# A transformer block's gradients on one core: the second norm made again in the tail, filters loaded twice, three pairs of w_down turned by TensorE

## The chip, the cores and the metric

The kernel runs on one core of a Trainium2 chip. The metric is the time of one execution on the device in microseconds. Five engines appear: TensorE (PE, with its weight loads as PEld), VectorE (DVE), ScalarE (ACT), GpSimd (POOL) and SyncE (SP). SP and POOL issue all of the kernel's transfers (DMAs).

## The reference

All data are bf16: 2048 tokens (S) of width 576 (D), a hidden width of 4608 (F).

```python
sa, ca, ga, sb, cb, gb = six rows of (silu(c) @ w_mod)
h = layernorm(x) * (1 + ca) + sa
x = x + ga * irfft2(rfft2(h) * (w_r + 1j * w_i))       # x1 below
h = layernorm(x) * (1 + cb) + sb                        # the second norm
x = x + gb * (((h @ w_gate) * (h @ w_up)) @ w_down)
```

The kernel gives this block's output and, for a given grad_out, the gradients of x, w_r, w_i, w_gate, w_up, w_down, c and w_mod. Both norms are over the 576 elements of a token. The filters w_r and w_i have 2048 x 289 elements.

## The kernel before, in words

Tokens are taken in 16 tiles of 128 (t), the hidden width in 36 blocks of 128 (fb). Four parts follow one another.

**Head** (0 to 62 us of the profile): loads, first norm, first transforms of the spectral filter. The two filters are loaded into one SBUF tile wn (L520, L521), whose rows are padded from 289 to 292 by a memset, and the padded tile is stored to a DRAM scratch wn_d (L524) for the tail.

**u4 and the forward filter** (62 to 268 us): u4 is (grad_out x gb) times w_down transposed, 36 blocks of four groups (function `u4_group`). PE needs w_down with its 576 columns on the partitions. So two blocks of w_down rows at a time (a pair k, 18 in all, buffer wdn, two of them) are loaded by SP (`wd_load`, L375 and L376) and turned by a DMA transpose, also from SP (`wd_turn`, L380, tile wdT). The groups of u4 are dealt between the steps of the filter (its stages 2 and 3); the blocks from 23 on run alone, at 4.1 us each, with the last 64 of 576 columns ahead (L549) and the others after them (L554). Stage 3 makes x1, stores it, and makes the second norm pair by pair of token tiles (`s3_norm`): ACT scales x1 to n2 (L669), DVE makes h2 from it in h2p (L671 to L673), POOL stores n2 (L674) to a scratch n2_d for the tail. Each four token tiles, SP transposes h2p to h2T by DMA (L677), which the main loop reads. n2 is laid out as six parts of 96 columns with two ones after each (98 wide, and padding to 608); with the ones, a matmul against it also gives column sums.

**Main loop** (268 to 1231 us): the 36 blocks of gate, up and their gradients.

**Tail** (1231 us on): in stage 1 the gradient goes back through the second norm (`t1_norm`, `norm_back`), one token tile a step, 16 steps of 4.0 us. SP loads n2 (tile n2c, five buffers) and y (yc, three buffers) of each tile (L1089). In `t1_turn`, `t1_cols` and `t1_rows` PE transposes (trp), and makes two transforms (zp, vp), with ACT copying each result out of PSUM (gyT, zt, b_Vp); csA, csB and csC gather the sums for the gradients of the modulation. The projection by w_down (u3p, L1394) is dealt between these steps and the later ones; its weights wd and its inputs hl are loaded as memory comes free (`queued_load`), by POOL and SP. Stage 2 multiplies by the filter, which POOL loads back from wn_d (L1176), with Xn, the stored spectrum, for the filter gradients (gwt, L1234). Stage 3 goes back to tokens and through the first norm.

The order on PE and ACT in the tail is written out by hand (`deal`, `in_order`). On SP and POOL a scheduler orders the instructions by priorities; `behind` and `queued` add an order between named instructions. Each queue issues in order: an instruction that waits holds all that stand behind it on its engine.

Of the kernel before, what the change touches and what calls it, by code (L numbers as in the profile page):

```python
# [10 lines left out]
BF = mybir.dt.bfloat16  # L11
# [14 lines left out]
DN = 608  # L26
# [64 lines left out]
def build(ctx, tc, A_x, A_w_r, A_w_i, B_w_gate, B_w_up, B_w_down, c_in, w_mod, grad_out,  # L91
# [25 lines left out]
    wn_d = dram("wn_d", [128, 2 * NT * FP], BF)  # L117
    n1_d = dram("n1_d", [128, NT, D], BF)
    n2_d = dram("n2_d", [128, NT, DN], BF)
# [7 lines left out]
    rstd2g = glob.tile([128, NT], FP32, name="rstd2g")  # L127
    dsl_col = glob.tile([128, 5], FP32, name="dsl_col")
# [5 lines left out]
    def part(ap):  # L134

        return ap[:, 0:6 * (DS if ap.shape[-1] == DN else DC)].rearrange("p (m c) -> p m c", m=6)[:, :, 0:DC]

    def parts(ap):

        return ap[:, :, 0:6 * (DS if ap.shape[-1] == DN else DC)].rearrange("p t (m c) -> p t m c", m=6)[:, :, :, 0:DC]  # L140
# [5 lines left out]
    def ones_between(ap):  # L146

        nc.gpsimd.memset(ap[:, :, 0:6 * DS].rearrange("p t (m c) -> p t m c", c=DS)[:, :, :, DC:DS], 1.0)
        nc.gpsimd.memset(ap[:, :, 6 * DS:DN], 1.0)
# [30 lines left out]
    def norm_stats(xt, pool, nt, name, rstd_out, room=None):  # L180
# [9 lines left out]
        nmr = pool.tile([128, room or nt], FP32, name=name + "_nmr")  # L190
        nc.vector.scalar_tensor_tensor(out=nmr[:, 0:nt], in0=mv[:, 0:nt, 0], scalar=-1.0, in1=rstd_out, op0=MUL, op1=MUL)
        return nmr
# [80 lines left out]
    with ExitStack() as hs:  # L273
# [95 lines left out]
        turns, wdTs = [], {}  # L369
# [8 lines left out]
        def wd_turn(k, pool):  # L378
            wdTs[k] = pool.tile([128, FB4, 5, 128], BF, name="wdT")
            turns.append(nc.sync.dma_start_transpose(out=wdTs[k][:].rearrange("q j m f -> q (j m) f"), in_=wdn2[:, k % 2, :, :].rearrange("f j d -> f (j d)")).ins)  # L380
# [25 lines left out]
        for k_ in range(2):  # L406
            wd_turn(k_, u4w)
# [116 lines left out]
        nc.gpsimd.dma_start(wn_d, wn[:].rearrange("k c a f -> k (c a f)"))  # L524
# [11 lines left out]

        def u4_group(g, eng=None):
            fb, sb4 = g // 4, g % 4
            k, j = fb // FB4, fb % FB4 if fb < NFB - FB4 else NFB - 1 - fb
            if k not in wdTs:  # L540
                wd_load(k)
                wd_turn(k, u4w if not u4r or k % 5 < 2 else u4r[0])
            if sb4 == 0:
                sts[fb] = ghh0 if fb == NFB - 1 else (u4w if not u4r or fb % 4 < 2 else u4r[1]).tile([128, NT, 128], BF, name="ghh_st", bufs=2)
            if fb >= TWICE and sb4 == 0:
                pts = [(fps if fb % 2 else u4ps).tile([128, 4, 128], FP32, name="u4p", tag="fp" if fb % 2 else "u4p") for _ in range(3)] + [fps.tile([128, 4, 128], FP32, name="u4p", tag="fp")]
                for q in range(4):
                    r = slice(64 * (q % 2), 64 * (q % 2) + 64)
                    nc.tensor.matmul(pts[q][:], lhsT=wdTs[k][r, j, 4, :], rhs=goT[r, 4 * q:4 * q + 4, 4, :], start=True, stop=False)  # L549
                u4r[2:] = pts  # L550
            pt = u4r[2 + sb4] if fb >= TWICE else u4ps.tile([128, 4, 128], FP32, name="u4p")
            n = 4 if fb >= TWICE else 5
            for m in range(n):
                nc.tensor.matmul(pt[:], lhsT=wdTs[k][:, j, m, :], rhs=goT[:, 4 * sb4:4 * sb4 + 4, m, :], start=(m == 0 and n == 5), stop=(m == n - 1))  # L554
# [83 lines left out]
        n2r = [hw2.tile([128, 2, DN], BF, name="n2r%d" % k, bufs=1) for k in range(2)]  # L638
        for n_ in n2r:
            ones_between(n_[:])  # L640
# [15 lines left out]
        def s3_norm(sa):  # L656
# [5 lines left out]
            n2 = n2r[sa // 2 % 2]  # L662
# [4 lines left out]
            nmr2 = norm_stats(x1, hw2, 2, "ln2", rstd2g[:, s0:s0 + 2])  # L667
# [3 lines left out]
            nc.vector.tensor_tensor(out=h2.rearrange("p t (m c) -> p t m c", m=6), in0=parts(n2[:]), in1=twice(modh[MCB][:]).rearrange("p t (m c) -> p t m c", m=6), op=MUL)  # L671
# [240 lines left out]
    with ExitStack() as ts:  # L912
# [44 lines left out]
        ones_b = tl.tile([128, 128], BF, name="ones_b")  # L957
        gsc = tl.tile([128, 5, 6], FP32, name="gsc")
# [9 lines left out]
        def norm_back(pool, gn, n, rstd, res, out, name):  # L968
# [3 lines left out]
            w = pool.tile([128, D], BF, name="w" + name, bufs=1)  # L972
# [10 lines left out]
        def deal(held, proj):  # L983
            more, seq, acts = held + proj, list(lead), scaled["2"][0:3]
            for n, (stage, k, ins) in enumerate(staged):
                last_ = len(seq)
                seq += ins
                steps = sum(x[:2] == (stage, k) for x in staged)
                at = sum(x[:2] == (stage, k) for x in staged[:n + 1])
                q = 16 if stage == 1 else 12 if stage == 2 else 20 if k == 0 else 16  # L990
                q = q * at // steps - q * (at - 1) // steps
                seq, more = seq + more[:q], more[q:]
                if stage == 1:
                    own, fill = ([then_act[i_.name] for i_ in part_ if i_.name in then_act] for part_ in (ins, seq[last_ + len(ins):]))
                    acts += own + scaled["2"][k + 2:k + 3] * (at == max(1, steps - 1) and k > 0) + fill
# [37 lines left out]
        def spread(d, rows=None):  # L1033

            for h in range(2):
                k = slice(h * 288, (h + 1) * 288)
                pp = ps_fp.tile([128, 512], FP32, name="spp", tag="fp")
                mm = nc.tensor.matmul(pp[:, 0:288], lhsT=(ones_b if rows is None else ones_f)[:], rhs=(d if rows is None else rows)[:, k], start=True, stop=True)
# [29 lines left out]
        with ExitStack() as r1:  # L1068
# [8 lines left out]
            gxa = c1b.tile([128, D + 4], BF, name="gxa")  # L1077
            with tc.high_priority(HEAD_START):
                nc.vector.memset(rings["gxf"][:, :, D:DP], 0.0)
# [3 lines left out]
            def t1_norm(t):  # L1083
                if t == 0:
                    nc.sync.dma_start(ga_h[:], modb_d[:, MGA, :])
                for k, src, tt in [("n2c", n2_d, 0)] * (t == 0) + [("n2c", n2_d, t + 1)] * (t < NT - 1) + [("yc", y_d, t)]:
                    ld[k, tt] = c1.tile([128, DN if k == "n2c" else D], BF, name=k, bufs=5 if k == "n2c" else 3)
# [3 lines left out]
                if t in (1, 2):  # L1091
                    ld["order"] = [ins.ins]
                    with behind(ld["order"]):
                        for k, tag in ((("RF", "tA"),), (("G1", "tB"), ("BD2", None), ("BDA", None)))[t - 1]:
                            T[k] = load_table(tl0, k, tag)
                    ld["order"] = [tab_ins[k]]
                n2 = ld["n2c", t][:]
# [3 lines left out]
                with behind([summed[(8, 12, 15)[t]]] if t < 3 else []):  # L1101
                    norm_back(c1, gn, n2, rstd2g[:, t:t + 1], gon(t), gx, "2")
# [6 lines left out]
            def t1_turn(t):  # L1109
# [6 lines left out]
                n2c, yc = ld["n2c", t], ld["yc", t]  # L1116
# [35 lines left out]
            for t, k in zip((5, 6, 7, 9, 9, 11, 11, 15, 15, 15), (0, 1, 3, 4, 5, 6, 7, 9, 8, 10)):  # L1152
                seq += [i_ for i_ in [ld["n2c", "ins", t]] if i_ not in seq] + late_sp[k]
# [40 lines left out]
        def wn_load(c, behind_):  # L1194
            queued(nc.gpsimd, behind_, wn[:, c].rearrange("k a f -> k (a f)"), wn_d[:, c * NT * FP:(c + 1) * NT * FP])
# [16 lines left out]
        queued_load(13, wn_load, 0)  # L1212
        queued_load(14, wn_load, 1)
        with behind([last[nc.gpsimd]]):
            gb_h = modh(MGB, "gb_h", gbhp, nc.gpsimd)
            nc.gpsimd.memset(ones_b[:], 1.0)
            nc.gpsimd.memset(gsc[:], 0.0)
# [80 lines left out]
        for n_ in n1cs:  # L1298
            ones_between(n_[:].unsqueeze(1))
# [51 lines left out]
        secp = pool("secp", 1, "right", stack=rA)  # L1351
        hlp = pool("hlp", 4, "right", stack=rA)
# [19 lines left out]
        for tp_ in range(NT // 2):  # L1372
# [4 lines left out]
            with behind([last[nc.gpsimd]] if tp_ == 0 else []):  # L1377
# [56 lines left out]
        for m0, w in ((0, 4), (4, 1)):  # L1434
            pp = ps_fp.tile([128, 512], FP32, name="gcp", tag="fp")
            nc.tensor.matmul(pp[:, 0:w * 128], lhsT=ones_b[:], rhs=gcd[:, m0:m0 + w, :].rearrange("p m n -> p (m n)"), start=True, stop=True)
# [63 lines left out]
```

## Time and profile before

| | |
|---|---|
| median of 3 | 1494.57 us (1494.44, 1494.57, 1502.95) |
| the profiled execution | 1508.15 us, its span 1506.3 us |
| mean granted clock of PE | 0.995 |
| DMA, mean over the span | 184 GB/s |
| h2T transposes in stage 3, us to landing (least, median, most) | 5.0, 14.1, 16.4 |
| wdT transposes from 150 to 270 us, the same | 3.7, 10.5, 18.2 |
| n2c loads in the tail, the same | 3.1, 5.5, 9.5 |
| Xn loads, 1320 to 1350 us, the same | 3.1, 7.7, 10.1 |

The span is the time from the first to the last instruction that the profile shows; times in it are microseconds from its start. In the timeline a line gives start, length, engine, line of the kernel, operation, output and inputs, how many instructions it stands for, and in brackets how long the engine had been idle and what ended that. SPq is SP's own queue: its length there is the time to issue a transfer, and the transfer lands later. L numbers are lines of the kernel before.

### The profile page before, as it was taken

The numbers are of one execution on the slowest core, as the hardware profiler recorded it, in microseconds if no ns is written. First come the engines' busy times: TensorE is split into PE (matmuls) and PEld (weight loads), VectorE is DVE, ScalarE is ACT, GpSimd is POOL, SyncE is SP. The second block draws the span as 40 slices with busy tenths as digits, with TensorE's granted clock in tenths as the row PEclk, the third lists the DMA queues.
The fourth block names the chain that finished last, engine by engine and source line by source line (L and its number), as shares of the span: only waits on it lengthen the run. The fifth ranks groups of instructions, "written<-read, shape, count | busy, mean of one in ns | idle before, by whom it ended". The sixth has DMA issues, their size and how long they took to land.

```text
span 1506.3 us, 29074 instructions
## 1 busy us (share of the span) xinstructions
PE 1473.0 (98%) x11189; PEld 1004.3 (67%) x11189; DVE 1054.0 (70%) x2642; ACT 557.2 (37%) x1168; POOL 243.0 (16%) x381
## 2 busy tenths in 40 slices
PE   7999997999999999999999999999999999999998
PEld 6665542566666666667667666666666667788776
DVE  6576762666777767767767677667677669778896
ACT  6666751322222222222222222222222225677740
POOL 1011221201101101102111111111111013221004
PEclk9999998999999999999999999999999999999999
DMA  9878999698877767768768668579578578995886
GB/s 330 269 223 211 261 237 199 158 154 161 170 142 161 159 126 166 156 121 171 154 126 183 137 128 188 127 142 171 130 141 186 104 161 248 282 315 170 235 284 175
DMA packets 498941, 277.16 MB, mean 184 GB/s; under 512 B 423025, under 2 KB 470642, under 8 KB 497778
## 3 DMA queue, kind: packets, MB, share of 16 engines
q1 hardware_dynamic: 470690, 172.24, 55.0%
q0 software_dynamic: 28112, 103.07, 23.3%
q8 instruction: 87, 1.43, 0.4%
q14 instruction: 52, 0.43, 0.1%
HBM read 105.90 MB, written 81.77 MB: 125 GB/s over the span
## 4 chain that ended last, share of the span: by engine, by line
PE 87%; DMA 5%; DVE 4%; issue 2%; ACT 1%; POOL 1%; SPq 0%; POOLq 0%; DVEq 0%
PE u57p L743 28%; PE u8p L846 19%; PE gup L810 17%; PE u4p L554 10%; PE u3p L1394 4%; PE gup L805 3%; PE yp L222 1%; DMA wdT<-wdn 1%; DMA h2p<-in_A_x_dram 1%; DMA gonA<-in_grad_out_dram 1%; PE zp L480 1%; DMA out_dram<-woT 1%; PE upa L215 1%; DVE pr L1066 1%; DMA woT<-so 1%
## 5 line engine op out<-in xcount | busy, mean ns | idle before, releaser
L851 DVE TENSOR_TENSOR acc<-acc,u8p 128x288 f32<-128x288 f32 (+1 forms) x1088 | 483.1, 452 | 276.1 <-PE u8p L846 272.6
L846 PE MATMUL u8p<-wT,ggT 128*128 128x288 bf16 x1152 | 328.0, 286 | 1.6 <-DVE acc L851 1.6
L846 PE MATMUL u8p<-wT,guT 128*128 128x288 bf16 x1152 | 327.6, 286 | 0.0
L810 PE MATMUL gup<-h2T,wgu 128*128 128x512 bf16 x1152 | 297.8, 379 | 0.0
L745 ACT CAST so<-u57p 128x288 bf16<-128x288 f32 x216 | 86.2, 399 | 525.0 <-PE u57p L743 509.9
L743 PE MATMUL u57p<-h2p,gu_sf 128*128 128x288 bf16 x1152 | 186.4, 286 | 0.0
L743 PE MATMUL u57p<-h2p,gg_sf 128*128 128x288 bf16 x1152 | 185.9, 286 | 0.0
L810 PEld LDWEIGHTS <-wgu 128*128 128x128 bf16 x1152 | 109.6, 98 | 97.9 <-issue 16.6
L846 PEld LDWEIGHTS <-ggT 128*128 128x128 bf16 x1152 | 112.6, 98 | 66.5 <-issue 14.0
L554 PE MATMUL u4p<-goT,wdT 128*128 128x512 bf16 x668 | 154.9, 383 | 0.0
L846 PEld LDWEIGHTS <-guT 128*128 128x128 bf16 x1152 | 112.7, 98 | 57.6 <-issue 2.4
L1394 PE MATMUL u3p<-wd,hl 128*128 128x288 bf16 x936 | 140.9, 286 | 2.8 <-DMA wd<-in_B_w_down_dram 2.8
L812 ACT CAST gT<-gup 128x512 bf16<-128x512 f32 x144 | 84.4, 586 | 131.5 <-PE gup L810 129.6
L743 PEld LDWEIGHTS <-hh_sf 128*128 128x128 bf16 x1152 | 112.7, 98 | 28.4
L743 PEld LDWEIGHTS <-gu_sf 128*128 128x128 bf16 x1152 | 112.5, 98 | 28.4
L743 PEld LDWEIGHTS <-gg_sf 128*128 128x128 bf16 x1152 | 112.5, 98 | 28.2
L1394 PEld LDWEIGHTS <-hl 128*128 128x128 bf16 x1152 | 107.4, 98 | 27.0 <-issue 3.9
L812 ACT CAST uT<-gup 128x512 bf16<-128x512 f32 x144 | 84.4, 586 | 77.5 <-PE gup L810 77.5
L554 PEld LDWEIGHTS <-wdT 128*128 128x128 bf16 x668 | 63.3, 99 | 74.2 <-issue 8.7
L743 PE MATMUL u57p<-gonC,hh_sf 128*128 128x288 bf16 x576 | 99.7, 286 | 0.0
L823 POOL DMA_DIRECT2D hhT_d<-hhT x36 | 33.3, 925 | 376.5 <-DVE hhT L814 333.6
L174 ACT CAST ghh_st<-u4p 128x512 bf16<-128x512 f32 x94 | 53.7, 589 | 63.6 <-PE u4p L554 63.0
(412 smaller groups left out, 1791.3 us busy)
## 6 DMA issues: line engine op xcount, KB each, us to landing
hhT_d<-hhT POOLq DMA_DIRECT2D x36, 512.0 KB, 6.3
ghhT_d<-ghh_st POOLq DMA_DIRECT2D x35, 512.0 KB, 5.1
ghh<-ghhT_d POOLq DMA_DIRECT2D x35, 512.0 KB, 7.3
hl<-hhT_d SPq DMA_DIRECT2D x28, 576.0 KB, 6.3
out_dram<-woT SPq DMA_DIRECT2D x70, 128.0 KB, 2.0
wdn<-in_B_w_down_dram SPq DMA_DIRECT2D x18, 288.0 KB, 4.2
wd<-in_B_w_down_dram POOLq DMA_DIRECT2D x36, 144.0 KB, 4.4
out_dram<-so SPq DMA_DIRECT2D x36, 144.0 KB, 2.9
```

The lines of the kernel that those rows point to most:

```text
L174: nc.scalar.copy(dst, src)
L215: nc.tensor.matmul(ps_a[:, fc, :], lhsT=A[:, c, sa, 128 * fc:128 * fc + 128], rhs=GB[:, sa, 1 - c:3 - c, :].rearrange("k v s -> k (v s)"), ...
L554: nc.tensor.matmul(pt[:], lhsT=wdTs[k][:, j, m, :], rhs=goT[:, 4 * sb4:4 * sb4 + 4, m, :], start=(m == 0 and n == 5), stop=(m == n - 1))
L743: mm = nc.tensor.matmul(pw[0][:, 0:288], lhsT=sf[:, t, :], rhs=rhs_n(t, h * 288, 288), start=(t == 0), stop=(t == NT - 1))
L745: followed(mm, nc.scalar.copy(so[:, h * 288:(h + 1) * 288], pw[0][:, 0:288]))
L805: nc.tensor.matmul(pts[-1][:], lhsT=wgu[r, 8, jw * 128:(jw + 1) * 128], rhs=h2T[r, 4 * sb4:4 * sb4 + 4, 4, :], start=True, stop=False)
L810: nc.tensor.matmul(pts[k][:], lhsT=wgu[:, 4 * wi_ + m, jw * 128:(jw + 1) * 128], rhs=h2T[:, ts_, m, :], start=False, stop=(m == 3))
L812: nc.scalar.copy((gT, uT)[wi_][:, th_, :], pts[k][:])
L823: nc.gpsimd.dma_start(hhT_d[:, :, fb, :].rearrange("tp f x -> f tp x"), hhT[:].rearrange("f (tp ti) p -> f tp (ti p)", ti=2))
L846: nc.tensor.matmul(pu[:, 0:288], lhsT=l_, rhs=r_, start=(k == 0), stop=(k == len(mms) - 1))
L851: summed[t] = nc.vector.tensor_tensor(out=ghb(t)[:, hs_] if fbs[-1] == NFB - 1 else dst, in0=dst, in1=pu[:, 0:288], op=ADD).ins
L1394: mm = nc.tensor.matmul(p2[ti][:, 0:288], lhsT=hls[fb // 9][:, fb % 9, ti * 128:(ti + 1) * 128], rhs=w[:, fb - f0, h * 288:(h + 1) * 288], ...
```

## The change

Three parts, and what follows from them.

- The second norm's output n2 is no longer stored. Stage 3 makes it without ones between its parts, in a tile with two buffers; the negative mean times the reciprocal deviation of each token is kept (nmr2g). In the tail SP loads x1 (x1c, three buffers) instead of n2, and ACT makes n2 from it again, into four tiles n2s whose ones POOL has written once. The hand-written order of ACT places the tile for step k + 2 in step k.
- The scratch wn_d goes. The tail loads the filters from the inputs a second time, by two loads on SP instead of two on POOL, and POOL clears the padding.
- The pairs 13, 15 and 17 are not turned by DMA. PE turns them, ten 128x128 transposes each into PSUM (wdp), and DVE copies the result to wdT. They stand in the blocks 25, 29 and 33, after the first of the block's groups.
- Smaller: norm_back writes its product into the tile gxa instead of one of its own, ones_b becomes a view of the fp32 ones, gsc moves to a later pool, and a second load of x1 in stage 3 of the tail stands behind those before it.

```diff
+        PE_TURNED = (13, 15, 17)
         def wd_turn(k, pool):
             wdTs[k] = pool.tile([128, FB4, 5, 128], BF, name="wdT")
+            if k in PE_TURNED:
+                return
...
+        def wd_ready(k):
+            if k in wd_in:
+                return
+            wd_in.add(k)
+            wd_load(k)
+            wd_turn(k, u4w if not u4r or k % 5 < 2 else u4r[0])
...
-            if k not in wdTs:
-                wd_load(k)
-                wd_turn(k, u4w if not u4r or k % 5 < 2 else u4r[0])
+            wd_ready(k)
+            if sb4 == 0 and fb % 2 == 0 and k + 1 in PE_TURNED:
+                wd_ready(k + 1)
+            if sb4 == 1 and fb % 2 == 1 and k + 1 in PE_TURNED:
+                for i in range(FB4):
+                    pt = fps.tile([128, 5, 128], BF, name="wdp", tag="fp")
+                    for m in range(5):
+                        nc.tensor.transpose(pt[:, m, :], wdn2[:, (k + 1) % 2, i, wide(m)], ident[:])
+                    evac(wdTs[k + 1][:, i], pt[:], eng="v")
...
-        nc.gpsimd.dma_start(wn_d, wn[:].rearrange("k c a f -> k (c a f)"))
...
-                nc.scalar.activation(out=part(n2[:, i, :]), in_=part(x1[:, i, :]), func=ACT.Identity, bias=nmr2[:, i:i + 1], scale=rstd2g[:, s0 + i:s0 + i + 1])
+                nc.scalar.activation(out=n2[:, i, :], in_=x1[:, i, :], func=ACT.Identity, bias=nmr2g[:, s0 + i:s0 + i + 1], scale=rstd2g[:, s0 + i:s0 + i + 1])
...
-            nc.gpsimd.dma_start(n2_d[:, s0:s0 + 2, :], n2[:])
...
-            more, seq, acts = held + proj, list(lead), scaled["2"][0:3]
+            made, s2 = scaled["made"], scaled["2"]
+            more, seq, acts = held + proj, list(lead), made[0:2] + s2[0:1] + made[2:3] + s2[1:3]
...
-                    acts += own + scaled["2"][k + 2:k + 3] * (at == max(1, steps - 1) and k > 0) + fill
+                    acts += own + s2[k + 2:k + 3] * (at == max(1, steps - 1) and k > 0) + made[k + 2:k + 3] * (at == 1 and k > 0) + fill
...
+            n2s = [c1b.tile([128, DN], BF, name="n2s%d" % k) for k in range(4)]
...
-                for k, src, tt in [("n2c", n2_d, 0)] * (t == 0) + [("n2c", n2_d, t + 1)] * (t < NT - 1) + [("yc", y_d, t)]:
-                    ld[k, tt] = c1.tile([128, DN if k == "n2c" else D], BF, name=k, bufs=5 if k == "n2c" else 3)
+                wanted = [("x1c", x1_d, 0)] * (t == 0) + [("x1c", x1_d, t + 1)] * (t < NT - 1) + [("yc", y_d, t)]
+                for n_, (k, src, tt) in enumerate(wanted[::-1] if t == 2 else wanted):
+                    ld[k, tt] = c1.tile([128, D], BF, name=k, bufs=3)
...
+                n2 = n2s[t % 4][:]
+                made.append(nc.scalar.activation(out=part(n2), in_=part(ld["x1c", t][:]), func=ACT.Identity, bias=nmr2g[:, t:t + 1], scale=rstd2g[:, t:t + 1]).ins)
...
-            queued(nc.gpsimd, behind_, wn[:, c].rearrange("k a f -> k (a f)"), wn_d[:, c * NT * FP:(c + 1) * NT * FP])
+            queued(nc.sync, behind_, wn[:, c, :, 0:DF], (wr_v, wi_v)[c])
...
-        queued_load(13, wn_load, 0)
-        queued_load(14, wn_load, 1)
+        for c in range(2):
+            wn_load(c, ld["yc", "ins", NT - 1])
+        nc.gpsimd.memset(wn[:, :, :, DF:FP], 0.0)
```

More of the change, by code (lines that the diff above doesn't have):

```diff
@@ L1077, in build @@
             gxa = c1b.tile([128, D + 4], BF, name="gxa")
+            n2s = [c1b.tile([128, DN], BF, name="n2s%d" % k) for k in range(4)]
+            made = []
             with tc.high_priority(HEAD_START):
+                for n_ in n2s:
+                    ones_between(n_[:])
                 nc.vector.memset(rings["gxf"][:, :, D:DP], 0.0)
@@ L1090, in t1_norm @@
                     ld[k, "ins", tt] = ins.ins
[L1091 to L1097, printed above, removed]
+                    if t in (1, 2) and n_ == 2 - t:
+                        ld["order"] = [ins.ins]
+                        with behind(ld["order"]):
+                            for k, tag in ((("RF", "tA"),), (("G1", "tB"), ("BD2", None), ("BDA", None)))[t - 1]:
+                                T[k] = load_table(tl0, k, tag)
+                        ld["order"] = [tab_ins[k]]
+                n2 = n2s[t % 4][:]
+                made.append(nc.scalar.activation(out=part(n2), in_=part(ld["x1c", t][:]), func=ACT.Identity, bias=nmr2g[:, t:t + 1], scale=rstd2g[:, t:t + 1]).ins)
+                scaled["made"] = made
                 gh, gx = ghb(t), rings["gxr"][:, t % 4, 0:D]
@@ L1152, in build @@
             for t, k in zip((5, 6, 7, 9, 9, 11, 11, 15, 15, 15), (0, 1, 3, 4, 5, 6, 7, 9, 8, 10)):
-                seq += [i_ for i_ in [ld["n2c", "ins", t]] if i_ not in seq] + late_sp[k]
+                seq += [i_ for i_ in [ld["x1c", "ins", t]] if i_ not in seq] + late_sp[k]
             in_order(seq)
@@ L1376, in build @@
             x1t = o2p.tile([128, 2, D], BF, name="x1t3")
-            with behind([last[nc.gpsimd]] if tp_ == 0 else []):
+            with behind([last[nc.gpsimd]] if tp_ < 2 else []):
                 x1l = nc.gpsimd.dma_start(x1t[:], x1_d[:, 2 * tp_:2 * tp_ + 2, :])
```

52 lines of the change are left out of this document (24 added, 28 removed).

## The prediction, made before the changed kernel was run

> **What bounds the kernel now.** I read the page first: the busy shares, then the 40 slices.
>
> ```profile
> PE 1473.0 (98%) x11189; PEld 1004.3 (67%) x11189; DVE 1054.0 (70%) x2642; ACT 557.2 (37%) x1168; POOL 243.0 (16%) x381
> ...
> PE   7999997999999999999999999999999999999998
> ...
> PEclk9999998999999999999999999999999999999999
> ```
>
> TensorE (PE) is busy 98% of 1506.3 us. The only slice after the start in which both PE and its clock dip is the seventh (226 to 264 us). No edit takes matmuls away, so all there is to win are PE's few idle microseconds: 33.3 us in the span, a third of them in that slice. The list of waits names them:
>
> ```profile
> PE u4p L549 <- DMA wdT<-wdn: 9.7, 1, 9.7
> ...
> PE u3p L1394 <- DMA wd<-in_B_w_down_dram: 2.8, 1, 2.8
> ```
>
> Total, times, longest: one wait each. Around the first, the timeline of PE:
>
> ```profile
> 223.59 0.60 PE L549 MATMUL u4p<-goT,wdT 64*128 64x512 bf16 x4
> 224.12 3.63 PE L554 MATMUL u4p<-goT,wdT 128*128 128x512 bf16 x16
> 227.68 0.60 PE L549 MATMUL u4p<-goT,wdT 64*128 64x512 bf16 x4
> 228.22 3.63 PE L554 MATMUL u4p<-goT,wdT 128*128 128x512 bf16 x16
> 241.52 1.04 PE L549 MATMUL u4p<-goT,wdT 64*128 64x512 bf16 x4 [9.67 <-DMA wdT<-wdn]
> 242.49 5.72 PE L554 MATMUL u4p<-goT,wdT 128*128 128x512 bf16 x16
> 248.14 0.60 PE L549 MATMUL u4p<-goT,wdT 64*128 64x512 bf16 x4
> ```
>
> A block takes 4.10 us (223.59 to 227.68). The one after the wait took 6.62 (241.52 to 248.14), since the granted clock was 0.50 from 242 to 246: the wait costs 9.67 + 2.52 = 12.2 us. Counting on from 223.59 (block 28, pair 14), the block that waited is 30, the first of pair 15. Why it waited, from SP's timeline:
>
> ```profile
> 208.23 1.62 SPq L380 DMA_TRANSPOSE wdT<-wdn  x1
> 218.74 0.37 SPq L375 DMA_DIRECT2D wdn<-in_B_w_down_dram  x1
> ...
> 220.39 6.15 SPq L677 DMA_TRANSPOSE h2T<-h2p  x1
> 226.70 0.46 SPq L722 DMA_DIRECT2D opcb_h<-modb_d  x1
> 227.28 6.29 SPq L380 DMA_TRANSPOSE wdT<-wdn  x1
> ...
> 241.49 0.37 SPq L375 DMA_DIRECT2D wdn<-in_B_w_down_dram  x1
> ```
>
> Pair 14 was turned at 208.23 in 10.5 us, in time for 223.59. Pair 15's turn went out at 227.28, behind an h2T transpose, and took 14.2 us (the next load into its buffer left at 241.49).
>
> **Sum, against the profiled execution** (1508.15 us: span 1506.3 and 1.85 around it). It is 13.6 us (0.9%) above the median of 1494.57; I carry the difference over to the median unchanged. About 1% (15 us) is what a measurement of this kernel can tell from no change.
>
> **Pairs 13, 15, 17 turned by PE.**
> - Old wait gone: -12.2.
> - Added: 3 x 2 groups of five 128x128 transposes. The tail's trp group of five takes 0.44 us, and the next matmul starts 0.28 after its start: 6 x 0.28 to 0.44 = 1.7 to 2.6, all on PE's path; I take +2.2. The six copies from PSUM (128x640, 0.82 us each by the goT row of this form) go to DVE, which is busy 1.38 of 4 us in these blocks: hidden, 0.8 each if not. A page of the Trainium skill speaks against this part: TensorE: Matmul & The Clock Gate, section "Part 4: PE-mode transpose", gives about 275 ns for one transpose in a kernel; an estimate by it is 30 x 0.275 = 8.3 us, and the whole sum below would become +3.7. The trp rows disagree: 219 ns is the latency of one, five together take 0.28 to 0.44.
> - A new wait. In the changed SP queue h2T(1), h2T(2), opcb_h, two loads of wgu, h2T(3) and gb_l all stand ahead of the turn of pair 14. h2T(3) must wait for DVE's last second-norm sum, which ends at 210.80 (start 210.04, 0.76). Issue of h2T 5.9 (median of its four), gb_l 0.53: pair 14's turn leaves at 217.3 instead of 208.23. wdT's landings in this stage are 3.7/10.5/18.2 (least, median, most), so it lands at 221.0 to 235.5. The case closest to it, right behind an h2T just after the second norm, is the 14.2 above (231.5); with fewer stores by then I take halfway between 10.5 and 14.2: 12.4, 229.7. PE wants it at 223.59 + 0.7 (one turn of two groups) = 224.3. So a wait of 5.4 (0 to 11.2). Behind it on PE stands all of u4, and behind that the main loop, so nothing gives it back.
> - Clock after that wait: 2.5 lost after 9.67 idle, nothing visible after 2.84 idle (clock 1.00 from 1300 to 1320). 5.4 is nearer to the second, but the low clock is a state that comes whole: I take +2.5 (0 to 2.5). The Trainium skill (same page, section "HAM oscillation — how this bites in real kernels") puts the limit at an idle gap of about 3.4 us, which fits both waits; by it a wait of under 3.4 would be free of this term.
>
> Together -12.2 + 2.2 + 5.4 + 2.5 = **-2.1**. Pair 16 (next DMA turn) has four blocks, 16 us, after pair 14's landing, against at most 18.2 + a load of 4.2: no term, up to +6.
>
> **Second norm.** Eight stores of n2 (304 KB each) and four memsets leave POOL; stage 3 waits for neither: 0 (-1 to 0). In the tail 16 ACT operations are new. The same operation in stage 3 takes 860 ns, a pair 1.62. One step of tail stage 1 on ACT:
>
> ```profile
> 1284.12 0.71 ACT L1136 CAST b_Vp<-vp 128x292 bf16<-128x292 f32 x2
> 1285.25 0.72 ACT L1128 CAST zt<-zp 128x292 bf16<-128x292 f32 x2 [0.41 <-PE zp L1127]
> 1286.39 0.69 ACT L1114 COPY gyT<-trp 128x640 bf16<-128x640 bf16 x1 [0.42 <-PE trp L1112]
> 1286.98 0.78 ACT L971 ACTIVATE u<-gn,rstd2g 128x576 bf16<-128x576 bf16 x1
> 1287.66 0.19 ACT L971 ACTIVATION_READ_ACCUMULATOR u<-gn,rstd2g 128x1 f32 x1
> 1287.84 0.40 ACT L745 CAST so<-u57p 128x288 bf16<-128x288 f32 x1
> 1288.14 0.71 ACT L1136 CAST b_Vp<-vp 128x292 bf16<-128x292 f32 x2
> ```
>
> The step is 4.02 us with 0.83 idle; the new one needs 0.81, placed before zt. It moves zt by 0.4, which gyT's idle takes up. Take +0.5; if that cover fails 0.3 a step, 16 steps, +5. x1 replaces n2 in the loads, with three buffers instead of five; before, DVE waited 6.2 us in four times for n2, none of which shows in PE's waits. The first weight-gradient copy on ACT (so, 1238.73, next used 1246.09) moves behind three new operations: +0.5 (0 to 2).
>
> On SP the woT transposes are no longer held behind n2 loads that wait for csB. woT was issued at 1277.87 and stored at 1286.76; this store's landing released wd's load on POOL at 1298.16, and PE's second wait (2.84) ended at 1305.90. Some 4 us earlier, that wait goes: -2.8 (-2.8 to 0). PE's timeline has no other idle time from 1300 to 1312, so nothing stands just behind it.
>
> **Filters.** The store of 2336 KB at the start goes (0, -1 to 0). In the tail the two loads (1168 KB each, POOL, 1312.34 and 1313.40, landings 8.2 and 14.1 us) become two on SP, behind the last yc; their memory is free once DVE has read grad_out for the last time (L976, 1311.35). POOL now clears the filters' pad after both have landed, and the Xn loads (1322.39 before) stand behind that. Landing at 1311.4 + 11.2 to 14.1, + 0.23 for the memset (its row at the start), + Xn's 10.1 = 1332.9 to 1335.8; DVE wants Xn at 1333.08, and is busy 18.7 of 20 us in the stage that follows, so that a delay stays: 0 to 2.7, I take **+1.5**. The hl loads behind them (4.2 to 10.5 us) have PE's other u3 groups as cover: 0 (to +2).
>
> Tail: 0.5 + 0.5 - 2.8 + 1.5 = **-0.3**. All: **-2.4**, 1505.7 against the profiled execution, 1492 against the median.
>
> **Rivals.**
> - A: pair 14 lands in time (7.0 us or less from issue; the least landing was 3.7). For it: fewer stores run by then; against it: the median is 10.5, and the one right behind an h2T took 14.2. The wait and its clock term go: -2.4 - 7.9 = -10.3, 1484.
> - B: it takes the full 18.2: wait 11.2, so -2.4 + 5.8 = +3.4, 1498. The old wait only changed its pair.
> - C, slower: POOL's memset. The filter loads come as 2048 rows of 578 bytes instead of long rows per partition. With L from issue to landing the loss is 1311.4 + L + 0.23 + 10.1 - 1333.1 = L - 11.4. At the start of the kernel such loads landed in 8.1 and 13.6. From L = 15.3 the kernel is slower than before; at twice 14.1 the loss is 16.8, so -2.4 - 1.5 + 16.8 = +12.9, 1507.5.
> - D: ACT sets tail stage 1: +5 instead of +0.5, 1497.
>
> **How the numbers follow.** Forecast (-7 to +2) 0.45; A 0.18; B 0.13; C 0.15; D 0.09. No single case but C's far end, or several together, passes 1%: faster 0.04 (A with every other bound at its low end), same 0.86, slower 0.10. The range takes in A and most of C: 1482 to 1505.
>
> **What would show it.** Right: block 30 starts without a wait, block 28 waits about 5 us on wdT and the block after it takes over 6 us; the wait on wd in the tail is gone; tail stage 1 keeps a step of 4.0 us; the first gwt comes 0 to 3 us later after the last csB than before (11 us). Wrong: no wait in blocks 28 to 30 (A); the first gwt over 15 us after csB, with POOL idle ahead of the memset (C); PE waits on zt or gyT in each step (D).

## The result, and the profile after

The changed kernel took **1508.40 us** (median of 20 executions, 1500.02 to 1512.65), the kernel before beside it 1496.02 (20 executions, 1493.29 to 1519.03). The ratio of the two is 1.0059, with a 95% interval of 1.0036 to 1.0082: slower by about 9 us, and above the forecast's range of 1482 to 1505. It is within 1%, as the likeliest of the three chances had it, but the interval leaves no change out. The medians lie further apart than the ratio says: the changed kernel's times form two groups, nine from 1500.0 to 1505.0 and eleven from 1507.6 to 1512.7, and the median falls into the upper one.

The profiled execution of the changed kernel took 1503.27 us (span 1501.5), so it belongs to the lower group. Its page answers to the three lines shown of before: the busy time of each engine, and the slices of PE and of PE's clock.

```profile
PE 1475.8 (98%) x11219; PEld 1007.2 (67%) x11219; DVE 1058.2 (70%) x2648; ACT 567.6 (38%) x1184; POOL 236.3 (16%) x365
...
PE   7999999999999999999999999999999998999998
...
PEclk9999999999999999999999999999999999999999
```

30 PE operations more (3 pairs of two groups of five), 16 on ACT more, and 16 on POOL fewer. The dip of the seventh slice is gone. PE's list of waits (total, times, longest):

```profile
PE u8p L855 <- DVE acc L860: 5.0, 2, 4.7
...
PE u3p L1412 <- DMA wd<-in_B_w_down_dram: 1.6, 1, 1.6
...
PE csC L1021 <- DMA yc<-y_d: 1.1, 2, 0.7
```

No wait on wdT is left, old or new, and the one on wd is 1.6 instead of 2.8. At the head stands one that the prediction never named: 4.7 us of u8p behind DVE, at the start of the tail. Next, PE around the first of the three turned pairs, in the kernel after (start, duration, operation):

```profile
212.78 0.61 PE L562 MATMUL u4p<-goT,wdT 64*128 64x512 bf16 x4
213.32 1.04 PE L567 MATMUL u4p<-goT,wdT 128*128 128x512 bf16 x4
214.19 0.44 PE L554 MATMUL wdp<-ident,wdn 128*128 128x128 bf16 x5
214.47 0.59 PE L567 MATMUL u4p<-goT,wdT 128*128 128x512 bf16 x2
215.07 0.44 PE L554 MATMUL wdp<-ident,wdn 128*128 128x128 bf16 x5
215.35 2.32 PE L567 MATMUL u4p<-goT,wdT 128*128 128x512 bf16 x10
217.60 0.60 PE L562 MATMUL u4p<-goT,wdT 64*128 64x512 bf16 x4
...
225.80 0.61 PE L562 MATMUL u4p<-goT,wdT 64*128 64x512 bf16 x4
```

A block with a turn takes 4.82 us (212.78 to 217.60) instead of 4.10. Each group of five delays the next matmul by 0.28 (214.19 to 214.47), and ahead of the second group 0.17 is lost besides: the two matmuls from 214.47 need 0.43 at the pace of those before, and the group starts at 215.07. What it waits for there was not traced. The last line is block 28, the first of pair 14: it starts without a wait. SP's timeline shows why:

```profile
212.26 3.43 SPq L686 DMA_TRANSPOSE h2T<-h2p  x1
215.79 0.51 SPq L732 DMA_DIRECT2D gb_l<-modb_d  x1
216.36 3.22 SPq L377 DMA_TRANSPOSE wdT<-wdn  x1
...
223.56 0.37 SPq L370 DMA_DIRECT2D wdn<-in_B_w_down_dram  x1
```

Pair 14's turn left at 216.36, 0.9 before the forecast, and the next load into its buffer left at 223.56, 7.2 later: in time for 225.80. Last, ACT in one step of the tail's first stage:

```profile
1272.64 0.89 ACT L1112 ACTIVATE n2s<-x1c,nmr2g,rstd2g 128x576 bf16<-128x576 bf16 x1
1273.41 0.71 ACT L1144 CAST zt<-zp 128x292 bf16<-128x292 f32 x2
1274.32 0.69 ACT L1130 COPY gyT<-trp 128x640 bf16<-128x640 bf16 x1 [0.20 <-PE trp L1128]
```

The new operation stands ahead of zt, ACT still idles 0.20 before gyT (0.42 before), and the step stays at 4.01 us (gyT 1270.31 to 1274.32).

### The profile page after: what moved, and what is told of

It is laid out like the page before. It is cut to its first block, busy times and chain, and to the rows that moved or that the text cites. A ratio compares the mean times of both kernels' runs of the same rounds, so it can differ in the third digit from the quotient of the medians.

```text
span 1501.5 us, 29137 instructions
## 1 busy us (share of the span) xinstructions
PE 1475.8 (98%) x11219; PEld 1007.2 (67%) x11219; DVE 1058.2 (70%) x2648; ACT 567.6 (38%) x1184; POOL 236.3 (16%) x365
## 4 chain that ended last, share of the span: by engine, by line
PE 87%; DMA 6%; DVE 3%; issue 2%; ACT 1%; POOL 1%; SPq 0%; POOLq 0%; DVEq 0%; ACTq 0%
PE u57p L752 28%; PE u8p L855 19%; PE gup L819 17%; PE u4p L567 10%; PE u3p L1412 3%; PE gup L814 3%; PE yp L216 1%; DMA wd<-in_B_w_down_dram 1%; DMA h2p<-in_A_x_dram 1%; DMA gonA<-in_grad_out_dram 1%; PE zp L478 1%; DMA hl<-hhT_d 1%; POOL out_dram L1384 1%; DMA wo_l<-so 1%; PE upa L209 1%
```

## The experiments

Every version is split at four points that come in all of them: on PE the first matmul of the main loop (gup, at 256 to 260 us), the first csC of tail stage 1 and the last csC, and on DVE the first gwt. The table gives the stretches between them and to the end of the span, in the one profiled execution of each version, with the median and ratio of all its executions; the ratio is to the kernel before, executed beside it. The versions that only led from one step to the next stand in the text. The second column holds the head of the kernel with u4, the third the main loop and the tail's head, the fourth tail stage 1, the fifth the step that the filters and Xn end.

| version | head | to first csC | stage 1 | to gwt | rest | span | median | ratio to before (95%) |
|---|---|---|---|---|---|---|---|---|
| before_again | 256.4 | 989.2 | 67.2 | 11.0 | 172.5 | 1496.3 | 1494.46 | 0.9997 (0.9980 to 1.0014) |
| after | 260.0 | 993.8 | 64.4 | 11.5 | 171.8 | 1501.5 | 1508.40 | 1.0059 (1.0036 to 1.0082) |
| after_again | 260.1 | 994.9 | 71.9 | 11.6 | 171.8 | 1510.3 | 1508.00 | 1.0076 (1.0046 to 1.0105) |
| pe_only | 259.3 | 989.2 | 61.6 | 11.0 | 172.6 | 1493.7 | 1497.37 | 1.0026 (1.0013 to 1.0039) |
| norm_only | 256.8 | 992.9 | 71.6 | 11.0 | 172.4 | 1504.8 | 1506.89 | 1.0066 (1.0044 to 1.0088) |
| filt_only | 256.6 | 989.2 | 62.1 | 12.0 | 172.3 | 1492.2 | 1496.58 | 1.0012 (0.9994 to 1.0030) |
| ga_tab | 259.5 | 989.2 | 65.4 | 11.7 | 171.9 | 1497.7 | 1502.51 | 1.0047 (1.0027 to 1.0067) |
| yc4_ga | 260.0 | 989.2 | 69.8 | 11.7 | 172.2 | 1502.9 | 1500.59 | 1.0036 (1.0019 to 1.0052) |
| plain_wo | 260.0 | 993.4 | 61.1 | 12.4 | 172.9 | 1499.8 | 1500.37 | 1.0024 (1.0006 to 1.0041) |
| no_pe | 257.5 | 989.2 | 61.5 | 12.0 | 171.8 | 1491.9 | 1493.64 | 0.9996 (0.9981 to 1.0012) |

So three places cost time: the head (+3 to 4 us, wherever pairs are turned by PE), the tail's head (+4 to 6, wherever the second norm's part is in and nothing mends it), and stage 1, which differs by up to 11 us from one profiled execution to another. The theories, and the rivals of each:

- **The exception**: the wait of 12.2 us that the change was to remove stood in the one profiled execution of before, not in the median. Its rival: it stands in every execution, and the change put as much elsewhere.
- **ga_h** (theory G): a small load of SP, which DVE needs at the start of the tail, stands behind x1's loads and the tables. Its rival: DVE is late for n2s, which ACT now makes.
- **The loads of y** (theory Y): in stage 1 they are held on SP behind stores that wait for a turned woT. Its rivals are that three buffers are too few, and that the transfers themselves are slow because DMA transposes run among them (theory T).

### Both kernels once more

No edit.

> The kernel before once more. Theory E (the profiled execution of before was an exception): no wait above 2 us on wdT in the u4 blocks after the second norm, the main loop starts about 12 us earlier than 268.6, and the time lies near 1495. Rival U (the wait is there in every execution): a wait of 9 to 10 us on wdT again, main loop from 268, and the gain there must have been lost elsewhere in the changed kernel.

Measured: 1494.46 us, and a profiled execution of 1498.06. Its PE waits:

```profile
PE u3p L1394 <- DMA wd<-in_B_w_down_dram: 2.8, 1, 2.8
...
PE u8p L846 <- DVE acc L851: 1.6, 2, 1.3
PE csC L1012 <- DMA yc<-y_d: 1.5, 1, 1.5
```

No wait on wdT. Of the 20 executions of before beside the changed kernel only three lie above 1503 (1508.47, 1511.25, 1519.03), and none of the 12 here is above 1501. The profiled execution that the prediction was summed against was such an exception: it lay 13.6 us above the median, and the wait with its clock was 12.2 of that (the main loop starts at 268.6 there, at 256.4 here). The execution profiled here, which lacks the wait, still lies 3.6 above the median of its twelve. What the other slow executions of before lost is not known, since they have no trace.

> The changed kernel once more. Its twenty times lie in two groups, 1500 to 1505 and 1507 to 1513. Theory G (DVE waits in the last sums for ga_h, which stands behind three loads of x1 on SP): the wait of DVE on ga_h is there again, 4 us or more, with PE waiting as long on DVE's sum; if the second group is drawn this time, the wait is 8 to 12 us. Rival W: the second group has a wait on wdT in u4 instead, and ga_h costs the same as before.

Measured: 1508.00, and a profiled execution of the upper group, 1512.02. Two lines head its PE waits:

```profile
PE csC L1021 <- DMA yc<-y_d: 8.0, 1, 8.0
PE u8p L855 <- DVE acc L860: 5.0, 2, 4.7
```

The wait on ga_h is in both groups; the one on y sets this execution apart from the lower one. In it stage 1 is 71.9 us long, 4.6 longer than in before_again: y +6.55 (8.04 against 1.49) and +2.54 of clock behind it (6.55 us from that csC to the next instead of 4.01), less the wait on wd (2.79) and its clock (the granted clock was 0.50 from 1295 to 1297 us and 0.73 from 1297 to 1299, 1.5 lost), makes 4.8.

### The three parts, each alone

Each is the kernel before with only the hunks of one part: norm_only the second norm from x1, pe_only the three pairs by PE, filt_only the filters.

> The kernel before with the second norm's part alone (n2 made again from x1 in the tail, with the small memory changes that make room); filters and the turning of w_down as before. Theory G: ga_h stands behind the loads of x1 here too, so this part alone has most of the loss, ratio 1.004 to 1.008. Rival (the loss is in u4 or in the filters): ratio 0.999 to 1.002.

Measured: 1506.89. Its PE waits are the two of the changed kernel:

```profile
PE csC L1003 <- DMA yc<-y_d: 8.1, 1, 8.1
PE u8p L837 <- DVE acc L842: 4.1, 2, 3.8
```

Ten of its 12 times lie from 1505.9 to 1511.9, two at 1496.4 and 1497.1. This part alone gives the whole loss, in both places. The three parts alone (this one and the next two) add up to 1.04%, more than the 0.6 to 0.8% of the whole, so they do not simply add.

> The kernel before with the pairs 13, 15 and 17 turned by PE and nothing else. Both theories on the tail expect no more than the 30 transposes: 6 groups of 0.3 to 0.44, so +2 us and a ratio of 1.000 to 1.003, unless wdT waits of 2 us or more appear in u4 (that would be the prediction's new wait on pair 14: +5 to +8).

Measured: 1497.37, ratio 1.0026. The head is 2.9 longer, no wait on wdT appears, and the tail is no worse (u8p 1.6 in all, as in before_again, 0.3 on wd, none on y). The part costs its own work and removes nothing, in this execution or in the median.

> The kernel before with the filters' part alone (no store of the padded filters, two loads from the inputs in the tail, padding cleared by POOL). All theories on the tail expect it near the kernel before, ratio 0.999 to 1.002, with the first product of the filter gradients 0 to 2 us later after the last sums; rival C of the prediction (POOL's memset holds the loads of Xn): 3 us or more.

Measured: 1496.58, ratio 1.0012, not distinguishable from no change. From the last csC to the first gwt it took 12.0 us against 11.0.

### ga_h

In the kernel before (before_again) the load of ga_h is the first of its group on SP:

```profile
1221.40 1.23 SPq L1085 DMA_DIRECT2D ga_h<-modb_d  x1
```

In the changed kernel the scheduler has it behind six loads of x1, three of y and four tables:

```profile
1226.07 3.19 SPq L1103 DMA_DIRECT2D x1c<-x_d  x3
...
1231.22 1.25 SPq L244 DMA_DIRECT2D T_G<-tab_G  x1
...
1233.83 1.99 SPq L1103 DMA_DIRECT2D x1c<-x_d  x3
1235.99 0.39 SPq L1098 DMA_DIRECT2D ga_h<-modb_d  x1
```

DVE's first multiplication by ga_h waits for it, and PE behind DVE (the brackets give the idle time before and what ended it):

```profile
1243.27 0.46 DVE L1121 TENSOR_TENSOR gxa<-gxr,ga_h 128x576 bf16<-128x576 bf16 x1 [4.53 <-DMA ga_h<-modb_d]
```

```profile
1244.14 0.40 PE L855 MATMUL u8p<-wT,ggT 128*128 128x288 bf16 x1 [4.71 <-DVE acc L860]
```

From the first wait of u8p to the first csC PE took 17.30 us, against 12.75 in before_again: 3.45 of longer waits, the rest clock. The first try put ga_h ahead of the first load of x1 by an order between the two:

```diff
- nc.sync.dma_start(ga_h[:], modb_d[:, MGA, :])
+ ga_l = nc.sync.dma_start(ga_h[:], modb_d[:, MGA, :])
  ...
- with behind(ld["order"]):
+ with behind(ld["order"] + ([ga_l.ins] if t == 0 and n_ == 0 else [])):
```

> The changed kernel, with the first load of x1 put behind the load of ga_h, so that ga_h stands first on SP as in the kernel before. Nothing is left out. Theory G: the wait on ga_h and PE's wait on DVE in the last sums go, 5 to 10 us less than the changed kernel, 1496 to 1500, ratio to before 0.998 to 1.004. Rival (the ACT operations of tail stage 1, or x1's three buffers, are the cost): less than 2 us are won, ratio 1.004 to 1.008 stays.

Measured: 1515.60, ratio 1.0128, slower still. It was no test of the theory: the scheduler kept ga_h where it was and moved the loads of x1 behind it, so that x1's first tiles too came after the tables. u8p waited 3.27, and y 1.05, 7.22 and 5.55. The next one ties only the fourth tile of x1 (`k == "x1c" and tt == 3` as the condition):

> The changed kernel with one edit: the load of ga_h stands ahead of the loads of x1 for tiles 3 to 5 on SP instead of behind them; the order is otherwise the same. Theory G: DVE's wait on ga_h (4.5) and PE's wait on DVE's sums (4.7) fall to the 1.3 of the kernel before, which takes 3 to 4 us from both groups of times: 1496 to 1502 and 1504 to 1509, median near 1504. Rival: what is won there is lost to later loads of x1, and the median stays at 1508.

Measured: 1504.90, ratio 1.0074. ga_h went out 2.1 earlier, at 1233.91, but the wait stayed:

```profile
1241.64 0.46 DVE L1121 TENSOR_TENSOR gxa<-gxr,ga_h 128x576 bf16<-128x576 bf16 x1 [3.85 <-DMA ga_h<-modb_d]
```

In the trace's records of single transfers, T_G's load, issued just ahead at 1231.12, landed at 1240.87, and ga_h (144 KB) at 1241.55, 7.6 us after its issue. So what counts is the place against the tables, and the third try puts the tables behind ga_h:

```diff
- nc.sync.dma_start(ga_h[:], modb_d[:, MGA, :])
+ ga_l.append(nc.sync.dma_start(ga_h[:], modb_d[:, MGA, :]).ins)
  ...
- ld["order"] = [ins.ins]
+ ld["order"] = [ins.ins] + ga_l
```

> The changed kernel with the load of ga_h ahead of the tables T_RF and T_G on SP (in the earlier try it still stood behind T_G, and DVE's wait on it only fell from 4.5 to 3.9). Theory G: DVE's wait on ga_h goes, PE's wait on DVE in the last sums falls from 4.7 to about 1.3, 3 to 4 us less than the changed kernel whatever the waits on y do: least time about 1497, median about 1504. Rival: PE's wait stays above 3 for another reason (DVE's order), no gain.

Measured: 1502.51, ratio 1.0047. DVE does not wait any more:

```profile
1237.25 0.45 DVE L1121 TENSOR_TENSOR gxa<-gxr,ga_h 128x576 bf16<-128x576 bf16 x1
```

The stretch to the first csC is 989.2 us again, as in before. Four of its times lie from 1498.0 to 1499.5 and four from 1505.5 to 1507.4: both groups of the changed kernel moved down, and there are still two. ACT's n2s is in this version as it is in the changed kernel, so DVE's wait was ga_h's and not n2s's.

### The loads of y

In the kernel before (before_again), SP has both loads of y ahead of the stores that wait for woT:

```profile
1271.04 0.38 SPq L1089 DMA_DIRECT2D yc<-y_d  x1
...
1272.52 0.32 SPq L1089 DMA_DIRECT2D yc<-y_d  x1
1274.84 0.39 SPq L762 DMA_DIRECT2D out_dram<-woT  x1
```

In the changed kernel x1's loads run two tiles further ahead (x1's tile 9 is loaded beside y's tile 5; in before n2's tile 9 was loaded beside y's tile 7), the stores are tied to them, and one y stands behind the stores. After_again:

```profile
1269.43 1.55 SPq L764 DMA_TRANSPOSE woT<-so  x1
1271.03 2.25 SPq L1103 DMA_DIRECT2D x1c<-x_d  x1
1273.37 0.38 SPq L1103 DMA_DIRECT2D yc<-y_d  x1
1274.82 0.32 SPq L1103 DMA_DIRECT2D x1c<-x_d  x1
1281.99 0.39 SPq L771 DMA_DIRECT2D out_dram<-woT  x1
1282.43 0.66 SPq L772 DMA_DIRECT2D out_dram<-woT  x1
1283.20 1.18 SPq L1103 DMA_DIRECT2D yc<-y_d  x1
```

```profile
1295.86 0.56 PE L1021 MATMUL csC<-yc,gxr 128*128 128x96 bf16 x5 [8.04 <-DMA yc<-y_d]
```

The buffer of that last load came free at 1276.01. SP issued it at 1283.20 (held 7.19), and it landed at 1295.82 (12.62 more). With three buffers, 11.6 us lie between the release of a buffer and the need of the tile that comes into it. So two delays add up, and the next runs tell them apart. The first takes the hold away by tying the stores to loads of y instead of x1:

```diff
- for t, k in zip((5, 6, 7, 9, 9, 11, 11, 15, 15, 15), (0, 1, 3, 4, 5, 6, 7, 9, 8, 10)):
+ for (w_, t), k in zip((("x1c", 5), ("x1c", 6), ("x1c", 7), ("yc", 7), ("yc", 7), ("yc", 9), ("yc", 9), ("x1c", 15), ...
```

> The changed kernel with one edit in the hand-written order of SP: the stores of the two woT transposes stand behind the loads of y 7 and 9, as in the kernel before, instead of behind the loads of x1 9 and 11 (where the loads of y 6 and 8 stood behind the stores). Nothing is left out. Theory Y (a store that waits for woT's landing holds a load of y, and PE waits for that y up to 8 us): PE's wait on y falls under 2 us, the group of times above 1507 goes, median 1500 to 1503. Rival C (transfers are slow in that stretch anyhow, and y is late whatever stands ahead of it): the two groups stay, median 1506 to 1509.

Measured: 1507.47, ratio 1.0088, no gain. The two loads were held for 0.03 us, and took 13.2 and 13.1 from issue to landing: more than the 11.6 without any hold. PE still waited on y, 2.14 and 1.49. The next one joins this edit and that of ga_mid:

> The changed kernel with the two edits together. Theories Y and G: 1496 to 1500, ratio to before 1.001 to 1.004, what remains being PE's turning of three pairs (2 us) less what is saved at wd. Rival C: still two groups, median above 1503.

Measured: 1508.31, ratio 1.0086. u8p waited 3.61 and y 2.36; that y was held for 0.64 and took 13.5. The hold alone is not the cause. Four buffers instead of three for y, paid for by a ring of three instead of four for gxr:

```diff
- rings = {... (("gxr", 4, D), ("gxf", 3, DP))}
+ rings = {... (("gxr", 3, D), ("gxf", 3, DP))}
  ...
- ld[k, tt] = c1.tile([128, D], BF, name=k, bufs=3)
+ ld[k, tt] = c1.tile([128, D], BF, name=k, bufs=3 if k == "x1c" else 4)
```

> The changed kernel with four buffers for y's loads instead of three, for which the ring of x1's gradients (gxr) gives up one of four. A load of y then may leave four steps (16 us) ahead instead of three (11.6 us from release to need). Theory M (three buffers leave 11.6 us, and the loads take 9 to 13.5 in that stretch, held or not): PE's waits on y go, both groups of times become one, 1499 to 1503. Rival Y alone (the hold behind woT's stores decides): the hold of up to 8 us plus a landing of 9 to 12 still exceeds 16 at times, and a second group stays.

Measured: 1502.45, ratio 1.0046, and one group of times (1500.8 to 1504.7). The wait on y is gone, but not the slow loads: one of y took 16.1, and x1's tiles, which have three buffers, came late to ACT, behind which PE waited 2.45 at vp. The wait of u8p was only 1.88 here, with ga_h landing 2.5 earlier than in after, though this edit does not touch it. With ga_tab's edit added:

> The changed kernel with both edits, ga_h ahead of the tables and four buffers for y. Theories G and M: 1495 to 1499, ratio to before 1.000 to 1.004; what is left is PE's turning of three pairs (+2.2) less the wait on wd that shrinks. Rival: above 1500, something in tail stage 1 that has not been named.

Measured: 1500.59, ratio 1.0036; six times from 1496.1 to 1499.3, six from 1501.9 to 1507.2. The profiled execution is one of the upper six. The head of PE's waits, and the line of ACT's:

```profile
PE vp L1150 <- ACT zt L1144: 5.4, 1, 5.4
```

```profile
ACT n2s L1112 <- DMA x1c<-x_d: 18.3, 5, 9.0
```

The wait has moved from y (1.6 are left) to x1: in this execution too some load takes longer than its buffers cover. What makes the loads slow? SP's turns of the last wo tiles are DMA transposes, and they run among them; one, issued at 1275.93, was done at 1291.24. The test copies these last four tiles by a plain DMA, in the changed kernel and without the edits above. It leaves these blocks of two outputs unturned, so it serves for timing alone:

```diff
- late_sp.append([nc.sync.dma_start_transpose(out=woT[:], in_=so).ins])
+ turned_ = nc.sync.dma_start_transpose(out=woT[:], in_=so) if fb_ < NFB - 2 else nc.sync.dma_start(woT[:].rearrange("q m f -> q (m f)"), so)
+ late_sp.append([turned_.ins])
```

> The changed kernel in which the last four weight-gradient tiles (the last two blocks of w_gate's and w_up's gradients) are copied by plain DMAs of the same bytes where they were turned by DMA transposes, so these blocks of two outputs are left unturned; the order on SP is the same. Theory T (a DMA transpose next to the loads of the tail makes all of them slow, 12 to 20 us to landing): loads of y land in 5 to 8, PE's wait on y goes, the group above 1507 goes: 1499 to 1503. Theory B (the bytes in flight, or the three buffers alone, decide): waits on y of 8 us and two groups of times stay, median 1506 to 1509.

Measured: 1500.37, ratio 1.0024, and one group (1498.2 to 1502.1). PE waits neither on y nor on wd; the head of its waits is ga_h's, which this version does not mend:

```profile
PE u8p L856 <- DVE acc L861: 4.6, 2, 4.3
```

The list of DMA issues from 1268 to 1300 us gives the median time from issue to landing in its last column. First yc4_ga, then plain_wo:

```profile
wd<-in_B_w_down_dram POOLq DMA_DIRECT2D x1, 1152.0 KB, 17.5
x1c<-x_d SPq DMA_DIRECT2D x6, 144.0 KB, 15.9
yc<-y_d SPq DMA_DIRECT2D x6, 144.0 KB, 17.7
```

```profile
yc<-y_d SPq DMA_DIRECT2D x9, 144.0 KB, 6.4
...
wd<-in_B_w_down_dram POOLq DMA_DIRECT2D x1, 1152.0 KB, 9.1
x1c<-x_d SPq DMA_DIRECT2D x6, 144.0 KB, 7.5
```

Loads on SP and on POOL take half as long. In the whole of stage 1 no y took more than 8.6, against 12.6 in after_again and 20.4 in yc4_ga. Stretches of 15 us (after the busy times of the engines: granted clock, DMA share, GB/s), after_again first:

```profile
1270.00:1285.00 15.00, 15.00 (x166) 12.52 (x165) 13.46 (x38) 14.27 (x34) 4.48 (x8) 1.00 1.09 235
```

```profile
1270.00:1285.00 15.00, 15.00 (x160) 12.37 (x157) 13.29 (x38) 14.40 (x34) 5.26 (x8) 1.00 0.96 323
```

With the transposes the engines are as busy and move 235 GB/s (225 in yc4_ga), without them 323. The hold behind the stores shrinks as well here, since a plain copy is done sooner; but yc_first had taken the hold away with the transposes in place, and its loads still took 13. So the transposes are part of the cause. They are not all of it: the longest y load of stage 1 took 11.6 in before_again, 8.4 in pe_only and 9.6 in no_pe, with the same four transposes. One part of the delay shows in the landings: in seven traces (before_again, after, after_again, pe_only, yc4_ga, plain_wo, no_pe) no transfer of SP issued from 1226 to 1312 us lands before one that SP issued ahead of it. In after_again the transpose of 1269.43 landed at 1281.98, and the load of x1 issued at 1271.03 behind it at 1282.17. By these landings, which the profile infers from the semaphores, a slow transpose holds back the loads behind it.

### Without the turns by PE

Both mends (yc4_ga), with `PE_TURNED = ()`: the second norm's and the filters' part without the pairs.

> The same with no pair turned by PE (the list of pairs empty), so the second norm's and the filters' parts with both edits and u4 as before. If PE's turns are a plain cost of 2 to 3 us in the usual execution: 2 to 3 us below the kernel with turns, 1492 to 1496, and no wait on wdT in the profile. If they pay for themselves by sparing waits on wdT: as slow or slower than with them.

Measured: 1493.64, ratio 0.9996 (0.9981 to 1.0012). Ten of 12 times lie from 1492.6 to 1495.2, two at 1501.9 and 1504.2. PE waits neither on y nor on ga_h, and 0.2 on wd. It is 7 us quicker than yc4_ga, while the pairs alone cost 3 to 4 (pe_only); the other 3 to 4 go to the waits of stage 1 by the table (61.5 against 69.8, where yc4_ga's profile is of its upper group), which this version mostly escapes with the same transposes. What it shares with before_again and the versions with turns do not is the time at which stage 1 starts (1246.7, and 1245.6 in before_again, against 1248.5 and later). That this offset is what lets the loads miss the transposes was not tested, and alone it cannot be: pe_only starts at 1248.5, and the exceptional execution of before at 1257.8, and PE waits for y in neither. No version that was run beats the kernel before beyond its interval.

## Why the prediction was wrong

Two steps failed. The larger is "Second norm": its terms came to -1.8 (0.5 + 0.5 - 2.8), and this part alone costs 0.66%, some 10 us (norm_only). The other is the pairs: -2.1 was forecast, and they cost 0.26%, some 4 us (pe_only). That the whole stayed within 1% does not speak for the sum, which had the wrong sign.

**"I carry the difference over to the median unchanged" failed, and with it "Old wait gone: -12.2".** The prediction saw that its profiled execution lay 13.6 us above the median, and did not ask whether the wait it was about to remove was that difference. It was: before_again has no wait on wdT, and pe_only, which is this part alone, is slower by 0.26%. Against the median the term is 0, in the one trace of before_again and by pe_only's times.

**"A new wait" on pair 14, +5.4, and "+2.5" of clock: wrong, 0 and 0.** The turn left when it should (216.36 against 217.3), but was through in 7.2 us, not 12.4. Rival A had this for u4. The old landing of 14.2, taken as the closest case, came from the same exceptional execution. So -12.2 and +7.9 are both 0, and of -2.1 for u4 the +2.2 of the turns is left.

**"6 x 0.28 to 0.44 ... I take +2.2": right**, 3 x 0.72 = 2.16 us, so the rows held. The estimate of 8.3 by the Trainium skill (TensorE: Matmul & The Clock Gate, section "Part 4: PE-mode transpose") does not agree with it. The head as a whole grew by 2.9 (pe_only) to 3.7 (after_again); the 0.8 to 1.6 us beyond the turns were not traced to a wait, and versions without turns differ by up to 1.1 there (no_pe).

**"Second norm": the term is missing.** The prediction counted the stores, ACT's operations and the first `so`, and did not ask what else on SP stands behind x1's loads, which now come in another order. ga_h is a load that the diff does not touch; moved, it costs 3.45 us of waiting and 1.1 of clock in after, and 5.7 in all in after_again, where the clock stayed low twice as long. ga_tab, with ga_h ahead of the tables, has none of this.

**"-2.8" for wd, "Some 4 us earlier, that wait goes": right in the small and wrong in the sum.** The wait on wd fell from 2.79 to 1.63 in after and to nothing in after_again, where PE came some 8 us later because of y. That the earlier turns did this is not shown: it is 0.3 in pe_only and 0.9 in filt_only, which leave the second norm as it was. And what lets the woT turns go earlier is that they are tied to x1's loads, which run two tiles ahead, and that put the stores behind them ahead of a load of y. The prediction noted three buffers instead of five for x1 and looked no further at y, whose three buffers had no room left in before_again either (a wait of 1.49; the execution that the prediction was made from has none). Where loads and transposes meet badly, as in after_again, this costs 8.04 - 1.49 and 2.54 of clock.

**ACT, "+0.5": right** in kind, 0; the step stays 4.01 and rival D is refuted. **Filters, "+1.5": about right**, +0.5 to +1.0 from the last csC to gwt; in after the second filter load took 13.3 us, POOL's clearing of the pad started at 1321.84, 0.1 after its landing, the Xn loads landed in 5.6 to 6.1 instead of 10.1, and DVE waited 0.3 for Xn, which refutes rival C. That C's far end, 1507.5, comes near the measured median is luck: its cause is not there.

The sum, by the table, for after_again against before_again: head +3.7, tail's head +5.7 (of which 4.55 is what after shows from u8p to csC), stage 1 +4.6, filters +0.6, rest -0.7: +13.9, the difference of the spans but for rounding. Against the median the loss in stage 1 is larger, since before_again has waits there too (67.2, against 61.6 in pe_only). For after, of the lower group: +3.6, +4.6, -2.8, +0.5, -0.7 = +5.2.

What stays open: which meeting of loads and transposes puts an execution into the upper or the lower group, and so why no_pe and before mostly stay out of it.

## What to carry to other kernels

Before a wait of one profiled execution is priced as a gain, compare that execution with the median of the others: if it lies above by about that wait, the wait is the exception. When loads on a queue change their kind or number of buffers, list everything that the scheduler now places behind them, small loads that the diff does not name above all, and what each of those releases. A DMA transpose that is hidden itself can still be paid for by the loads beside it, so check the landings of loads with few buffers.

## What the runs showed of the hardware

- **Loads beside DMA transposes.** 144 KB loads took up to 20.4 us with four transposes of a wo tile among them, at most 8.6 with plain copies in their place, and a load issued by POOL slowed alike (17.5 against 9.1 for 1152 KB). With the same four transposes pe_only's loads of y took at most 8.4: the transposes slow the loads in some meetings and not in others. That POOL's own load slows too agrees with the Trainium skill (DMA: Bandwidth & Descriptors, section "Issuing engines are not separate DMA queues"), which has the transfers of all issuing engines run on the same 16 DMA engines.
- **A small load behind a large one.** ga_h landed 0.7 us after a table issued 2.8 ahead of it on the same queue (1241.55 and 1240.87), 7.6 after its own issue.
- **The clock falls after short idle times too.** The prediction saw none lost after 2.84 idle, and the limit of about 3.4 us of the Trainium skill (TensorE: Matmul & The Clock Gate, section "HAM oscillation — how this bites in real kernels") seemed to fit. The runs show otherwise: the granted clock fell to 0.50 for 3.41 us, by the traces' clock records, around 1.88 us of idle PE in yc4 (1242.6 to 1246.0), 2.14 in yc_first (from 1297.3), 2.79 in before_again and 3.27 in ga_first (1242.1 to 1245.5), and stayed at 1.00 after 1.63 in after, 2.45 in yc4 (at 1291) and 2.84 in before. Here the measurement decides: whether 2 to 3 us of idle cost clock or not differs from one execution to the next. Such a fall cost 1.5 us in before_again and 1.1 in after, and after 8.04 us of idle 2.54 in after_again.
